# Attention and soft mixture of experts in one kernel: one-operand vector operations, the gate in the norms' rows, four query buffers, a new written order

## The chip, the cores and the metric

One NeuronCore of a Trainium2 chip runs the whole program. The metric is the device time of one execution in microseconds (us), the median of three runs. The engines named below are PE (TensorE: matmuls, and with PEld its weight loads), DVE (VectorE), ACT (ScalarE), POOL (GpSimd) and SP (SyncE, which here only issues DMAs). Each engine works through its own instructions in order and waits where a semaphore tells it to.

## The reference

Batch 8, 8 heads, 576 positions, 64 features a head; then a soft mixture of 8 experts with 4 slots each. All is float32.

```python
scores = softmax_causal(q @ k.T / 8)                     # per (batch, head): 576 x 576
local  = scores @ v
q_p    = phi(q)                                          # phi(x) = x + 1 for x > 0, else exp(x)
mem    = (q_p @ M_prev) / (q_p @ z_prev + 1e-6)
g      = 1 / (1 + exp(-beta))                            # one gate for a head
x      = (g * mem + (1 - g) * local)                     # 4608 rows of 512
logits = x @ phi_moe                                     # 4608 x 32
d      = softmax over the 4608 rows;  slots = d.T @ x    # 32 x 512
slot_out = relu(slots @ w1[e]) @ w2[e]                   # 512 -> 1024 -> 512, per expert
out    = softmax over the 32 slots(logits) @ slot_out    # 4608 x 512
```

## The kernel before

**The attention.** The loop runs over 32 pairs of heads, n = 0 to 31 (8 batches, 4 pairs). A pair's work is cut into small operations, each a function `op_...`. Queries and keys are split on POOL into a rounded part and the rest (`qhi`, `qlo`, `kn`, `kl`, lines 396 to 406). PE multiplies them in three passes (`sA`, `sa`, `sB`, lines 408 to 429). DVE adds the mask and takes the row's extreme (`max`, line 450), ACT makes the exponential with its row sum (`exp`, line 458). PE transposes the blocks (`t`, line 551), ACT or DVE copies them out of PSUM (`te`, lines 364 and 367), and PE multiplies them with v (`av`, line 578).

**The memory branch.** ACT and DVE make phi(q) (`qmin`, `qexp`, `qphi`, lines 488 to 497) in one of three buffers `qp`. PE makes the norms (`norm`, line 503); `neps`, `nmk`, `nred` (lines 508 to 519) turn them into reciprocals, which go by a small DRAM tile `nd` (three of them, used in turn) into 17 rows of a tile `nG`. The row sums are scaled by the gate and inverted by `rec` (lines 464 and 465), transposed (`rt`), and multiplied by `nG` in `rf` (line 473). The product goes through DRAM (`rrw`) and comes back broadcast over 64 partitions as `FR` (`rrr`, line 483). `qn` (line 532) multiplies phi(q) with `FR` before PE uses it in `av.A` and `ava`, and `mo` and `xe` (lines 608 and 613) multiply the result with `FR`'s second half.

**The gate.** ACT makes exp(beta) and exp(-beta) at the start. In DRAM the second half of each `nd` is filled with ones by three DMAs that ACT issues (line 353).

**The first expert steps** run between: `x1` to `x4` (lines 618 to 681) keep a running maximum (`x1m`, line 635), a running denominator (`x1d`, line 648) and the slots' sums (`x4a`) over chunks of 512 rows.

**What sets the order.** `SEQ` (from line 34) writes out all operations in one list by hand or by search; each engine gets its instructions in that list's order and keeps it (`pin`). A table `EV` names the engine of each operation that more than one could do. A helper `turn` (line 843) makes DVE and POOL take turns on eight kinds of operation that read two tensors from SBUF, or feed such ones (`qhi`, `qlo`, `kn`, `kl`, `qphi`, `qn`, `nmk`): where the list goes from one engine to the other, the second waits for the first.

**The tail.** Weights come in pieces of 0.5 MB: 45 during the attention, 19 more when slots of the first layer come free. The first layer (`f1`) is followed by the second (`f2`, line 906), one call for each half of the model's features dh, group of experts and half of the hidden units. Then `comb(dh, t4)` (line 956) multiplies 512 rows with the slots' outputs, ACT and DVE copy the halves out of PSUM (three buffers `pp`), and a DMA writes. Nine blocks of 512 rows are done for dh = 0, then for dh = 1. For the first EARLY = 2 blocks each half of 256 features is written by itself (0.5 MB, line 960); the others are written whole, 1 MB, after dh = 1 (line 962):

```python
    for t4 in range(NQ):
        comb(0, t4)
        if t4 == 4:
            f2(1, 0, 1)
    f2(1, 1, 0)
    f2(1, 1, 1)
```

**The start.** `warm` has PE multiply zeros three times (WARM = 3, line 337) while the first loads are under way.

Of the kernel before, what the change touches and what calls it, by code (L numbers as in the profile page):

```python
# [39 lines left out]
exp.1h0@1 max.4h1@1 te.B3y@0 exp.4h0@1 max.1h1@1 loadq@3 sB@1 te.B3x@0 nrg@1 exp.a@1 te.B3@0 qphi@2 t.B2@0:0 qhi@2  # L40
t.B1@0:1 te.A2@0 te.B2@0 kn@2 max.2h1@1 te.B1@0 norm@2:2 rrr@0 max.2h0@1 qlo@2 exp.2h1@1 av.1@0 max.3h1@1 exp.2h0@1
neps@2 av.3@0 w.r2@0 max.3h0@1 exp.3h1@1 kl@2 av.2@0 exp.1h1@1 av.4@0 exp.3h0@1 nmk@2 exp.4h1@1 sA@2 nred@2 rec@1
nrw@2 sa@2 max.1h1@2 rt@1:0 t.B1@1:1 max.4h1@2 loadk@3 exp.1h1@2 t.B2@1:2 loadv@1 te.B1@1 max.4h0@2 qn.1@0 exp.4h1@2
t.A1@1:1 max.1h0@2 max.a@2 rf@1 sB@2 qn.0@0 rrw@1 te.A1@1 exp.1h0@2 ava@0:0 qmin@3 av.A@0 qhi@3 max.2h1@2 loadq@4
max.3h1@2 te.B2@1 kn@3 nrg@2 t.AA@1:1 xe@0 exp.4h0@2 mo@0 t.A3@1:2 qlo@3 t.A2@1:0 te.AAy@1 qexp@3 te.AAx@1 te.A3@1
t.B3@1:1 max.3h0@2 te.A2@1 kl@3 av.1@1 qphi@3 rrr@1 av.4@1 max.2h0@2 exp.2h1@2 norm@3:0 te.B3x@1 sA@3 exp.2h0@2 neps@3
te.B3@1 nmk@3 exp.3h0@2 te.A3y@1 nred@3 exp.a@2 sa@3 exp.3h1@2 t.A1@2:0 te.B3y@1 nrw@3 max.4h0@3 av.3@1 te.A3x@1
te.A1@2 loadk@4 av.2@1 rec@2 loadv@2 exp.4h0@3 max.1h1@3 rt@2:1 max.a@3 t.B2@2:2 rf@2 exp.1h1@3 max.1h0@3 t.A2@2:0
rrw@2 max.4h1@3 te.B2@2 t.B1@2:1 qn.0@1 qn.1@1 sB@3 loadq@5 te.A2@2 exp.4h1@3 w.r1@0 te.B1@2 ava@1:2 qmin@4 av.A@1
qhi@4 nrg@3 max.3h1@3 kn@4 qexp@4 xe@1 t.AA@2:0 mo@1 t.A3@2:1 qlo@4 exp.a@3 t.B3@2:2 qphi@4 rrr@2 av.1@2 max.3h0@3  # L50
te.B3@2 kl@4 te.B3x@2 max.2h1@3 av.3@2 te.A3y@2 w.r4@0 exp.1h0@3 max.2h0@3 av.2@2 exp.3h1@3 te.A3x@2 te.AAy@2 sA@4
te.A3@2 exp.2h1@3 exp.2h0@3 exp.3h0@3 sa@4 max.1h0@4 norm@4:1 loadk@5 max.1h1@4 te.B3y@2 av.4@2 rec@3 neps@4 loadq@6
t.B1@3:2 te.AAx@2 exp.1h1@4 max.4h0@4 nmk@4 rt@3:1 x3.1@c0:0 te.B1@3 rf@3 qn.0@2 max.4h1@4 exp.1h0@4 rrw@3 t.B2@3:1
x3e.1@c0 t.A1@3:2 max.a@4 nred@4 exp.4h0@4 sB@4 loadv@3 qn.1@2 te.A1@3 te.B2@3 nrw@4 exp.4h1@4 t.A2@3:0 max.2h1@4
qhi@5 qmin@5 ava@2:2 te.A2@3 av.A@2 kn@5 xe@2 exp.a@4 max.2h0@4 exp.2h1@4 t.AA@3:1 mo@2 qlo@5 t.B3@3:0 te.AAy@3
te.AAx@3 x3.0@c0:2 exp.2h0@4 max.3h0@4 rrr@3 t.A3@3:1 te.B3x@3 x3e.0@c0 kl@5 av.1@3 te.A3x@3 te.B3@3 te.A3y@3
max.3h1@4 qexp@5 av.3@3 nrg@4 te.A3@3 sA@5 qphi@5 te.B3y@3 loadv@4 exp.3h0@4 sa@5 w.r5@0 max.1h0@5 exp.3h1@4 norm@5:2
loadk@6 max.4h1@5 av.2@3 loadq@7 neps@5 max.1h1@5 exp.4h1@5 t.B1@4:1 max.a@5 nmk@5 max.4h0@5 t.B2@4:0 te.B1@4 rec@4
t.A1@4:2 qn.1@3 qn.0@3 rt@4:1 sB@5 rf@4 te.A1@4 te.B2@4 rrw@4 qmin@6 nred@5 av.4@3 qhi@6 ava@3:1 av.A@3 exp.4h0@5
max.3h0@5 nrw@5 qlo@6 xe@3 exp.1h1@5 max.2h0@5 w.r0@0 t.A2@4:2 qexp@6 mo@3 loadv@5 t.A3@4:0 exp.2h0@5 t.B3@4:1 kn@6  # L60
max.3h1@5 te.A3@4 av.1@4 te.A2@4 te.A3x@4 kl@6 te.B3x@4 te.A3y@4 exp.3h1@5 x1.0@c0:2 rrr@4 max.2h1@5 exp.a@5 te.B3@4
x1.1@c0 qphi@6 sA@6 x1l@c0 nrg@5 exp.3h0@5 x1m@c0 exp.2h1@5 t.AA@4:0 max.4h1@6 sa@6 te.AAy@4 norm@6:2 exp.1h0@5
loadk@7 av.4@4 max.4h0@6 neps@6 av.2@4 w.r6@0 te.B3y@4 max.a@6 nmk@6 max.1h1@6 te.AAx@4 t.B2@5:2 x1e@c0 max.1h0@6
nred@6 sB@6 exp.4h1@6 rec@5 nrw@6 te.B2@5 x1d@c0 qn.1@4 x2@c0:1 rt@5:0 qn.0@4 t.B1@5:2 av.3@4 rf@5 x2a@c0 max.3h0@6
te.B1@5 rrw@5 x4.0@c0:0 kn@7 qmin@7 max.3h1@6 x3.3@c0:1 qhi@7 x4a.0@c0 exp.1h1@6 ava@4:2 w.r3@0 av.A@4 xe@4 kl@7
exp.3h0@6 x3e.3@c0 loadq@8 exp.4h0@6 max.2h1@6 t.A2@5:0 loadv@6 max.2h0@6 t.A1@5:2 nrg@6 te.A2@5 qlo@7 mo@4 t.A3@5:1
te.A1@5 x3.2@c0:0 te.A3x@5 te.A3@5 t.AA@5:2 te.A3y@5 rrr@5 sA@7 qexp@7 te.AAy@5 x3e.2@c0 te.AAx@5 qphi@7 sa@7
max.1h0@7 exp.2h0@6 t.B3@5:1 loadk@8 max.4h0@7 exp.2h1@6 norm@7:2 av.1@5 max.a@7 neps@7 loadq@9 te.B3x@5 max.4h1@7
exp.3h1@6 nmk@7 av.2@5 max.1h1@7 te.B3y@5 te.B3@5 exp.1h0@6 av.4@5 nred@7 x4.1@c0:0 exp.a@6 exp.4h0@7 sB@7 rec@6 nrw@7
x4a.1@c0 qn.0@5 qn.1@5 rt@6:2 t.B2@6:1 rf@6 exp.1h1@7 t.A1@6:0 max.3h0@7 rrw@6 exp.4h1@7 t.B1@6:2 max.3h1@7 kn@8  # L70
av.3@5 exp.a@7 te.A1@6 qhi@8 av.A@5 exp.3h1@7 te.B2@6 qmin@8 qlo@8 ava@5:0 max.2h1@7 t.A2@6:1 loadv@7 xe@5 te.B1@6
mo@5 t.A3@6:0 nrg@7 exp.2h1@7 kl@8 t.B3@6:2 te.A2@6 exp.1h0@7 av.1@6 max.2h0@7 exp.3h0@7 rrr@6 te.A3x@6 te.B3y@6
te.A3y@6 sA@8 qexp@8 te.A3@6 te.B3@6 qphi@8 t.AA@6:1 sa@8 te.B3x@6 max.1h0@8 t.A1@7:0 exp.2h0@7 loadk@9 max.a@8
max.1h1@8 norm@8:2 max.4h0@8 exp.a@8 av.2@6 loadq@10 te.AAx@6 exp.1h0@8 rec@7 av.4@6 te.A1@7 neps@8 av.3@6 te.AAy@6
nmk@8 max.4h1@8 exp.4h0@8 rt@7:2 x3.1@c1:1 rf@7 t.B1@7:0 exp.4h1@8 nred@8 rrw@7 sB@8 qn.0@6 te.B1@7 x3e.1@c1 qn.1@6
nrw@8 t.A2@7:2 max.3h1@8 qhi@9 w.r8@0 qmin@9 ava@6:1 av.A@6 xe@6 kn@9 max.3h0@8 exp.1h1@8 te.A2@7 t.AA@7:0 mo@6 kl@9
t.A3@7:1 te.AAx@7 qexp@9 t.B3@7:2 te.AAy@7 max.2h0@8 rrr@7 exp.3h0@8 t.B2@7:0 max.2h1@8 qlo@9 av.1@7 te.B3@7 te.A3@7
te.B3x@7 te.B2@7 exp.2h0@8 av.3@7 te.A3y@7 nrg@8 exp.2h1@8 te.A3x@7 sA@9 qphi@9 te.B3y@7 exp.3h1@8 sa@9 max.1h1@9
x3.0@c1:0 loadk@10 max.4h1@9 exp.1h1@9 norm@9:1 loadv@8 x3e.0@c1 av.2@7 max.a@9 max.1h0@9 neps@9 max.4h0@9 t.A2@8:2
exp.4h1@9 nmk@9 rec@8 t.B1@8:0 qn.1@7 qn.0@7 rt@8:1 sB@9 rf@8 te.B1@8 te.A2@8 rrw@8 exp.4h0@9 ava@7:1 nred@9 av.4@7  # L80
qhi@10 av.A@7 qmin@10 max.3h0@9 nrw@9 kn@10 max.2h1@9 t.B2@8:0 qexp@10 loadv@9 qlo@10 xe@7 max.3h1@9 t.A1@8:2 te.B2@8
t.AA@8:1 mo@7 te.A1@8 x1.0@c1:0 kl@10 exp.3h1@9 te.AAx@8 te.AAy@8 x1.1@c1 max.2h0@9 t.A3@8:2 qphi@10 rrr@8 t.B3@8:1
x1l@c1 exp.2h0@9 te.A3y@8 sA@10 x1m@c1 exp.a@9 exp.1h0@9 nrg@9 te.B3y@8 exp.3h0@9 te.A3@8 sa@10 max.1h0@10 norm@10:0
exp.2h1@9 max.4h1@10 av.1@8 loadq@11 te.B3@8 loadk@11 max.1h1@10 te.B3x@8 neps@10 av.3@8 te.A3x@8 max.4h0@10
exp.1h1@10 nmk@10 av.2@8 x1e@c1 max.a@10 nred@10 av.4@8 exp.4h0@10 sB@10 rec@9 nrw@10 qn.0@8 qn.1@8 rt@9:1 x2@c1:0
t.B2@9:2 exp.4h1@10 x2a@c1 rf@9 x4.0@c1:0 max.3h0@10 rrw@9 qhi@11 te.B2@9 av.A@8 max.2h0@10 qmin@11 qlo@11 max.3h1@10
ava@8:2 loadq@12 exp.1h0@10 x4a.0@c1 x3.2@c1:1 loadv@10 xe@8 exp.3h0@10 t.B1@9:0 x3e.2@c1 kn@11 t.A2@9:2 exp.3h1@10
te.B1@9 t.A1@9:1 nrg@10 kl@11 te.A2@9 mo@8 x3.3@c1:0 te.A1@9 t.A3@9:2 max.2h1@10 qexp@11 t.AA@9:1 rrr@9 x3e.3@c1 sA@11
qphi@11 te.AAx@9 te.A3@9 te.AAy@9 sa@11 te.A3x@9 max.1h1@11 norm@11:0 exp.2h1@10 loadk@12 max.4h1@11 av.1@9 exp.2h0@10
# [983 lines left out]
```

## Time and profile before

| what | value |
|---|---|
| three timed runs | 505.86, 508.44, 504.3 us; median 505.86 us |
| the profiled execution | 502.58 us, of which span from first to last instruction 500.8 us |
| mean granted clock of TensorE | 0.951 of full speed |
| busy in the span | PE 440.7 us (88%), DVE 379.6 us (76%), ACT 333.1 us (67%), POOL 186.6 us (37%) |
| DMA | 97.11 MB, mean 194 GB/s |

The busy shares are means over unlike stages: a start in which little is loaded yet, 32 pairs of heads that look alike, an end in which the weights stream in, and a last stretch in which PE has nothing to do and the output is still being written. So the table tells which engine is close to full, and not yet what a change of one stage is worth.

### The profile page before, as it was taken

The page shows a single profiled execution, that of the slowest core. Times are in us where ns is not written, and L with a number is a line of the kernel's source. Part 1 is how long each engine was busy: PE and PEld are TensorE (multiplying, and loading weights), DVE is VectorE, ACT ScalarE, POOL GpSimd, SP SyncE. Part 2 cuts the span into 40 slices and gives each one's busy share as a digit, 9 for nine tenths or more (in the row PEclk, how much of TensorE's full clock was granted, in tenths as well). Part 3 has the DMA queues.
Part 4 walks back from the last instruction along what each step waited for, and adds up shares of the span by engine and source line. Part 5 has one row for each costly group of instructions (what it writes and reads, how often), then busy time and mean ns, then how long its engine had stood idle before and what let it go on. Part 6 is the DMA issues. An engine that isn't in the chain of part 4 may idle for free. (4 is left out here: it accounts for less than half of the span.)

```text
span 500.8 us, 13360 instructions
## 1 busy us (share of the span) xinstructions
PE 440.7 (88%) x4874; PEld 280.8 (56%) x4874; DVE 379.6 (76%) x1229; ACT 333.1 (67%) x956; POOL 186.6 (37%) x196
## 2 busy tenths in 40 slices
...
GB/s 137 84 161 126 264 206 187 193 145 144 135 176 203 177 106 171 134 237 199 174 164 194 168 219 161 175 175 140 239 150 170 131 161 327 394 411 328 21 335 335
DMA packets 40718, 97.11 MB, mean 194 GB/s; under 512 B 9014, under 2 KB 12366, under 8 KB 40654
## 3 DMA queue, kind: packets, MB, share of 16 engines
...
q8 instruction: 38, 0.62, 0.5%
...
## 5 line engine op out<-in xcount | busy, mean ns | idle before, releaser
L458 ACT ACTIVATE sm<-sm,nm 128x576 f32<-128x576 f32 (+4 forms) x288 | 166.3, 580 | 23.0 <-DVE nm L450 22.1
L450 DVE CUSTOM_DVE_ANT_0 sm<-psS,rm 128x192 f32<-128x192 f32 (+4 forms) x288 | 137.3, 509 | 11.8 <-PE psS L424 6.1
L578 PE MATMUL oa<-at,vv 128*32 128x512 f32 (+3 forms) x1280 | 114.9, 469 | 0.2 <-ACT at L364 0.2
L551 PE MATMUL psT<-cs,sm 128*128 128x128 f32 x768 | 109.4, 284 | 5.8 <-DVE rf L473 2.7
L364 ACT COPY at<-psT 128x512 f32<-128x512 f32 (+3 forms) x208 | 84.7, 419 | 42.9 <-PE psT L551 22.2
L551 PEld LDWEIGHTS psT<-cs,sm 128*128 128x128 f32 x768 | 86.1, 144 | 35.9 <-ACT at L364 5.6
L415 PE MATMUL psS<-K,X 64*128 64x256 f32 (+2 forms) x960 | 92.3, 327 | 7.1 <-DVE nm L450 4.8
L415 PEld LDWEIGHTS psS<-K,X 64*128 64x128 f32 x960 | 74.0, 190 | 26.8 <-issue 15.1
L367 DVE COPY at<-psT 128x256 f32<-128x256 f32 (+3 forms) x184 | 82.3, 458 | 8.6 <-ACT at L364 4.6
L532 POOL TENSOR_TENSOR at<-qp,FR 64x576 f32<-64x576 f32 x34 | 48.1, 1416 | 36.0 <-DMA FR<-rd 15.6
L458 ACT ACTIVATION_READ_ACCUMULATOR sm<-sm,nm 128x1 f32 x288 | 54.7, 190 | 0.0
L578 PEld LDWEIGHTS oa<-at,vv 128*32 128x32 f32 x1280 | 35.5, 109 | 31.5 <-issue 19.3
L514 POOL TENSOR_TENSOR rn<-rn,rm 128x144 f32<-128x144 f32 x27 | 11.7, 435 | 109.4 <-DVE rn L510 53.8
L406 POOL TENSOR_TENSOR K<-qk,K 128x576 fp32r<-128x576 f32 x32 | 45.4, 1419 | 3.4 <-DVE qp L497 1.9
L400 POOL TENSOR_TENSOR X<-qk,X 128x512 fp32r<-128x512 f32 x32 | 41.1, 1283 | 0.9
L369 POOL TENSOR_SCALAR X<-qk 128x512 fp32r<-128x512 f32 x32 | 19.9, 620 | 48.2 <-PE psS L415 33.7
L532 DVE TENSOR_TENSOR at<-qp,FR 64x576 f32<-64x576 f32 x30 | 22.3, 743 | 17.5 <-POOL at L532 14.3
L497 DVE SCALAR_TENSOR_TENSOR qp<-qk,qp 128x576 f32<-128x576 f32 x32 | 24.1, 752 | 12.0 <-ACT qp L493 7.3
L488 ACT ACTIVATE qp<-qk 128x576 f32<-128x576 f32 x32 | 21.9, 683 | 14.9 <-DVE at L532 12.3
L608 DVE TENSOR_TENSOR xt<-oa,FR 128x448 f32<-128x448 f32 (+7 forms) x60 | 23.8, 434 | 3.3 <-PE oa L578 3.2
L369 POOL TENSOR_SCALAR K<-qk 128x576 fp32r<-128x576 f32 x32 | 21.6, 675 | 9.0 <-DVE at L532 3.7
L450 DVE DVE_READ_ACCUMULATOR2_ANT nm<- 128x1 f32 x288 | 23.3, 81 | 0.0
...
## 6 DMA issues: line engine op xcount, KB each, us to landing
...
```

Source lines behind the costliest of these rows:

```text
L364: nc.scalar.copy(o, i)
L367: nc.vector.tensor_copy(out=o, in_=i)
L369: ENG = dict(a=act, v=dve, p=lambda o, i: nc.gpsimd.tensor_scalar(out=o, in0=i, scalar1=1.0, scalar2=1.0, op0=ALU.mult, op1=ALU.mult))
L400: nc.gpsimd.tensor_tensor(out=X[:, 1, :], in0=st[n]["q"][:, 64:576], in1=X[:, 0, :].bitcast(F32), op=ALU.subtract)
L406: nc.gpsimd.tensor_tensor(out=K2[:, 1, :], in0=kt[:, 0:S], in1=K2[:, 0, :].bitcast(F32), op=ALU.subtract)
L415: nc.tensor.matmul(ps[h][:, a:e], X[ROW[h], x, 128 * i - 128:128 * i], K2[ROW[h], y, k0:k0 + e - a], start=(x, y) == (0, 0), stop=(x, y) = ...
L450: nc.vector.tensor_tensor_reduce(out=smt(n, i, h), in0=src, in1=msk, op0=ALU.add, op1=ALU.min, scale=-0.125, scalar=3.0e38, accum_out=s["n ...
L458: nc.scalar.activation(sm, sm, AF.Exp, scale=-1.0, bias=s["nm"][:, J:J + 1], accum_out=s["sum"][:, J:J + 1])
L497: ALU_ENG[ev("qphi", n)].scalar_tensor_tensor(out=t, in0=st[n]["q"], scalar=0.0, in1=t, op0=ALU.max, op1=ALU.add)
L532: ALU_ENG[ev(f"qn.{h}", n)].tensor_tensor(out=C[r, h, :], in0=st[n]["qp"][r], in1=FR[r, 0:S], op=ALU.mult)
L551: nc.tensor.transpose(out=ps[:, 128 * x:128 * x + 128], in_=win(n, i, h, c), identity=ident)
L578: nc.tensor.matmul(o[r, c0:c1], vt[:, n % 2, c, r], rhs[h], start=start, stop=stop)
```

## The change

1. Three DVE operations lose one of two tensor operands. `rec` no longer multiplies by the gate (a `tensor_scalar` adds 1e-9). `x1m` and `x1d` take the running value as a per-partition scalar.
2. The gate of the local branch goes into the constant second half of the `nd` tiles, which are now four (one for a pair of heads in the batch). Six more DVE operations of `gate` and four DMAs that SP issues (`ndc`) fill them; ACT's three DMAs at the start are gone.
3. `qp` has four buffers in place of three.
4. WARM is 5, and three `wm` operations put 4 more multiplications of zeros among the first two pairs.
5. EARLY is 4. The `f2` calls of dh = 1 stand after 3, 6 and 9 blocks of dh = 0.
6. `SEQ` and `EV` are written anew. Counted in the two texts: `qn` on DVE 30 times before and 22 after, on POOL 34 and 42; `nmk` on DVE 5 and 1; `neps` on DVE 16 and 19; the copies `te`, `x1l`, `x2a` and `x3e` are shared differently at nearly the same sum. The list goes from POOL to DVE inside `turn` 62 times before and 38 times after; `qphi` on DVE comes directly behind a `qn` on POOL 18 times after and never before. From the last `qn` that frees a buffer to the `qmin` that wants it there were 3 to 19 entries of the list in between, and are 15 to 53.

```diff
-loadq@1 qhi@0 qmin@0 qlo@0 qexp@0 qphi@0 kn@0 gate@0 qmin@1 norm@0:0 neps@0 kl@0 nmk@0 qexp@1 nred@0 qphi@1 nrw@0 sA@0
-sa@0 max.1h1@0 norm@1:1 loadk@1 max.4h0@0 neps@1 loadv@0 max.a@0 max.1h0@0 exp.a@0 max.4h1@0 exp.1h1@0 sB@0 exp.4h1@0
+loadq@1 qhi@0 qlo@0 qmin@0 gate@0 kn@0 qexp@0 kl@0 ndc@0 qphi@0 norm@0:0 sA@0 neps@0 qmin@1 nmk@0 nred@0 qexp@1
+loadv@0 sa@0 max.4h1@0 loadk@1 nrw@0 max.4h0@0 exp.4h1@0 w.r0@0 max.1h0@0 max.1h1@0 loadq@2 exp.1h0@0 max.a@0 wm@2
 ...
-WARM = 3
-EARLY = 2
+WARM = 5
+EARLY = 4
 ...
-    qps = big.tile([128, 3, S], F32, name="qp")
+    qps = big.tile([128, 4, S], F32, name="qp")
 ...
-        for nd in nds:
-            nc.scalar.dma_start(out=nd[:, S:1088].rearrange("h (r x) -> h r x", x=128), in_=nG[0][0:8])
 ...
     def op_gate(n):
-        nc.vector.tensor_scalar(out=omg, in0=omg, scalar1=1.0e20, scalar2=1.0, op0=ALU.min, op1=ALU.add)
-        nc.vector.tensor_scalar(out=gc, in0=gc, scalar1=1.0, scalar2=None, op0=ALU.add)
-        nc.vector.tensor_scalar(out=epg, in0=gc[:, :, 12], scalar1=1e-6, scalar2=None, op0=ALU.mult)
+        nc.vector.tensor_scalar(out=ec, in0=ec, scalar1=1.0e-20, scalar2=None, op0=ALU.max)
+        nc.vector.tensor_scalar(out=epg, in0=ec, scalar1=1e-6, scalar2=None, op0=ALU.mult)
+        nc.vector.tensor_scalar(out=og, in0=og, scalar1=1.0e20, scalar2=1.0, op0=ALU.min, op1=ALU.add)
+        nc.vector.reciprocal(out=og, in_=og)
+        for a, b in ((0, 512), (512, S)):
+            nc.vector.tensor_scalar(out=at[0:8, a:b], in0=acc[0:8, 0:b - a], scalar1=og[0:8], scalar2=None, op0=ALU.add)
+
+    def op_wm(n):
+        ps = psO.tile([128, 512], F32, name="oa")
+        for i in range(n):
+            nc.tensor.matmul(ps, acc[:, 0:128], acc, start=True, stop=True)
+
+    def op_ndc(n):
+        for p in range(NP):
+            nc.sync.dma_start(out=nds[p][:, S:2 * S], in_=at[2 * p:2 * p + 2, 0:S])
 ...
-        nc.vector.scalar_tensor_tensor(out=f, in0=w(st[n]["sum"]), scalar=1e-9, in1=w(omg[:, n % NP, 0:12]), op0=ALU.add, op1=ALU.mult)
+        nc.vector.tensor_scalar(out=f, in0=st[n]["sum"].rearrange("a (h i) -> a h i", i=4), scalar1=1e-9, scalar2=None, op0=ALU.add)
 ...
-        nc.vector.tensor_tensor(out=mn, in0=mo, in1=mx, op=ALU.max)
+        nc.vector.tensor_scalar(out=mn, in0=mx, scalar1=mo, scalar2=None, op0=ALU.max)
 ...
-        nc.vector.scalar_tensor_tensor(out=den, in0=den, scalar=xs[qd]["al"], in1=xs[qd]["sm"], op0=ALU.mult, op1=ALU.add)
+        nc.vector.tensor_scalar(out=den, in0=den, scalar1=xs[qd]["al"], scalar2=xs[qd]["sm"], op0=ALU.mult, op1=ALU.add)
 ...
-    for t4 in range(NQ):
+    for t4 in range(3):
         comb(0, t4)
-        if t4 == 4:
-            f2(1, 0, 1)
+    f2(1, 0, 1)
+    for t4 in range(3, 6):
+        comb(0, t4)
     f2(1, 1, 0)
+    for t4 in range(6, NQ):
+        comb(0, t4)
     f2(1, 1, 1)
```

## Rows read from the trace of the kernel before

**Rows 1.** Windows by stage: busy us (count) of each engine, then PE clock, DMA share, GB/s
```profile
50.00:400.00 350.00, 322.27 (x3700) 212.87 (x3698) 308.60 (x1028) 274.71 (x809) 165.72 (x169) 1.00 0.62 176
456.00:475.70 19.70, 17.00 (x216) 9.34 (x214) 7.43 (x12) 6.68 (x13) 0.00 (x0) 1.00 0.31 112
475.70:500.80 25.10, 9.51 (x60) 6.01 (x58) 5.54 (x8) 4.32 (x8) 0.00 (x0) 0.50 0.92 334
```

**Rows 2.** Window of 4 us inside the last stretch
```profile
480.00:484.00 4.00, 4.00 (x28) 2.61 (x28) 2.08 (x3) 1.76 (x4) 0.00 (x0) 0.50 1.03 375
```

**Rows 3.** Chain that ended last, tail: start us, us, engine and line
```profile
458.41 0.66 PE pp L956 x8
...
463.30 1.86 PE pf L906 x32
465.17 0.66 PE pp L956 x8
...
468.74 3.63 PE pf L906 x64
```

**Rows 4.** Timeline of the start: start us, us, engine, line, operation, [idle before]
```profile
4.42 0.62 POOL L369 TENSOR_SCALAR X<-qk 128x512 fp32r<-128x512 f32 x1 [3.35 <-DMA qk<-in_q_dram]
...
4.83 2.45 ACTq L353 DMA_DIRECT2D nd<-nG  x3
...
7.32 0.68 ACT L488 ACTIVATE qp<-qk 128x576 f32<-128x576 f32 x1 [2.25 <-POOL X L400]
...
9.50 0.18 DVE L378 TENSOR_SCALAR rm<-rm 128x52 f32<-128x52 f32 x1
...
9.67 0.67 POOL L369 TENSOR_SCALAR K<-qk 128x576 fp32r<-128x576 f32 x1 [3.27 <-DVE qp L497]
9.68 0.71 PE L503 MATMUL psT<-qp,qk 128*32 128x144 f32 x8 [3.80 <-issue]
9.81 0.55 DVE L380 TENSOR_SCALAR rm<-rm 128x4 f32<-128x4 f32 x1
...
10.43 1.40 POOL L406 TENSOR_TENSOR K<-qk,K 128x576 fp32r<-128x576 f32 x1
...
11.88 2.02 PE L415 MATMUL psS<-K,X 64*128 64x256 f32 x14 [0.69 <-POOL K L406]
```

**Rows 5.** Window of the start's slow stretch, columns as in the first group
```profile
8.00:22.00 14.00, 10.88 (x64) 7.95 (x64) 8.64 (x31) 7.11 (x21) 4.73 (x6) 0.51 0.25 75
```

**Rows 6.** Single lines: engine, operation, duration ns min/median/max, first and last start
```profile
L464 DVE SCALAR_TENSOR_TENSOR r<-sum,rm x32: 110/171/1155, 23.6 to 401.0; 128x12 f32<-128x12 f32 x32
L648 DVE SCALAR_TENSOR_TENSOR den<-den,al,sm x8: 147/214/4619, 83.1 to 421.2; 128x1 f32<-128x1 f32 x8
L637 DVE TENSOR_SCALAR nmn<-mrun x8: 153/154/155, 80.0 to 417.0; 128x1 f32<-128x1 f32 x8
```

**Rows 7.** Timeline around the longest of line 648
```profile
171.10 4.62 DVE L648 SCALAR_TENSOR_TENSOR den<-den,al,sm 128x1 f32<-128x1 f32 x1
...
174.30 1.40 POOL L406 TENSOR_TENSOR K<-qk,K 128x576 fp32r<-128x576 f32 x1
```

**Rows 8.** Window behind it, columns as in the first group
```profile
172.00:180.00 8.00, 4.29 (x67) 3.06 (x66) 7.93 (x17) 3.77 (x12) 3.70 (x4) 0.92 0.04 6
```

**Rows 9.** Waits, summed: who waited for whom, us in total, times, longest
```profile
ACT qp L488 <- DVE at L532: 12.3, 12, 2.6
```

**Rows 10.** Groups by shape: xcount, busy us, mean ns, idle before
```profile
L532 POOL TENSOR_TENSOR at<-qp,FR 64x576 f32<-64x576 f32 x34 | 48.1, 1416 | 36.0 <-DMA FR<-rd 15.6 <-DVE nm L450 5.9 <-DVE r L464 4.4
L532 DVE TENSOR_TENSOR at<-qp,FR 64x576 f32<-64x576 f32 x30 | 22.3, 743 | 17.5 <-POOL at L532 14.3 <-DMA FR<-rd 2.8
L464 DVE SCALAR_TENSOR_TENSOR r<-sum,rm 128x12 f32<-128x12 f32 x32 | 10.4, 326 | 3.2 <-ACT sm L458 3.0
L337 PE MATMUL psT<-acc 128*128 128x512 f32 x6 | 4.4, 897 | 1.4 <-DVE acc L333 1.4
```

502 lines of the change are left out of this document (250 added, 252 removed).

## The prediction

> **What bounds the kernel now.** I read the stages first, then the tail's chain, the start's timeline, and last the small DVE operations one by one.
>
> In the windows by stage [rows 1] see three regimes. From 50 to 400 us PE is busy 322.27 of 350 us (92%) at full granted clock, DVE 308.60 (88%), POOL 165.72 (47%). PE's work is the same after the change, so at most its 27.7 us of idle time can be won there, and DVE is close enough to full that each stall of DVE can become one of PE. From 456 to 475.7 the DMA engines are busy 0.31 of the time. In the last 25.1 us PE has nothing left after 9.51 us: the output is being written, 334 GB/s x 25.1 us = 8.38 MB, which is 7 blocks of 1.05 MB and two halves; once it runs, the write holds 375 GB/s with the DMA share at its top [rows 2]. So the end is set by what is still to be written when dh = 1 begins, and the middle by PE with DVE close behind.
>
> **The change part by part.** The sum is against the profiled execution, 502.58 us, which lies 3.3 us under the median of the three runs, 505.86.
>
> *Tail writes (EARLY 4).* Two more halves of 0.52 MB are written during dh = 0, when the DMA engines are mostly free [rows 1]; four halves at 375 GB/s are 5.6 us and fit between the first block at 458.41 and 475.7 [rows 1, 3]. What remains is 7.34 MB, so 1.05 MB / 375 GB/s = 2.8 us off the end. PE makes a half each 9.51/9 = 1.1 us in that stretch [rows 1], 0.52 MB in 1.1 us being more than the DMA takes, so the supply doesn't limit. The new homes are pieces whose weights were used by the f2 calls of dh = 0; no wait is added. Bounds -1.5 (if two blocks must first collect) to -3.2 (at 334 GB/s). **-2.8.**
>
> *f2 between the blocks.* Five blocks took 463.30 - 458.41 = 4.89 us, four 468.74 - 465.17 = 3.57 [rows 3]: 0.94 a block, where the first of a group takes 0.66 of PE and the rest waits for copies. An f2 of 1.86 us [rows 3] lets all three PSUM buffers empty. Three groups of three at four fifths of 0.94 are 6.8 us, at 0.89 8.0, against 8.46. **-0.7**, bounds 0 and -1.7. It moves the first write of dh = 1, so it counts in full.
>
> *Start.* ACT issues three DMAs from 4.83 to 7.28 and its first `qmin` stands behind them until 7.32, though the query was there at 4.42 [rows 4]. That goes. But what is late next is POOL: in the new list the four splits come before `qphi`, so they end at about 4.42 + 0.62 + 1.40 + 0.67 + 1.40 = 8.5 (taking `qlo` as long as `kl`) instead of 11.83, and `qphi` waits for them by `turn`, with six small operations of the gate ahead of it on DVE (0.18 each [rows 4], so up to 1.1, and two longer ones that no row shows; 0 if they get done under POOL's work). With 0.74 for `qphi` from the nearest row [rows 10] and 0.71 for `norm` [rows 4] the scores start at 10.0 to 11.1, and all 18 passes, at 2.02/14 each, end at 12.6 to 13.7, against 13.9. The four `ndc` DMAs stand ahead of `loadv`, `loadk` and `nrw` on SP; at 2.45/3 each [rows 4] they cost SP 3.3 us, before any of those is wanted (`nrw` after `nred`, behind `norm`).
> The clock is the larger part. From 8 to 22 us it is granted at 0.51, the lower level of 1.2 GHz, after 3.80 us in which PE had nothing [rows 4, 5]. Two more multiplications of zeros ahead, 4.4/3 = 1.5 us each [rows 10], fill most of that gap and delay nothing. If the clock then stays at 2.4 GHz, 10.88 us of PE work become 5.4, a gain of up to 5.4 where PE is what is waited for. The four others cost up to 5.9 us at the lower clock, covered by the 3.1 us that PE is idle in that window: +2.8 if the clock stays low. Between -6.7 and +2.8 I take **-2**, nearer the row with the gap that gets filled, cut because DVE and ACT work 8.64 and 7.11 of those 14 us.
>
> *Small DVE operations.* The same `x1d` that takes 214 ns at the median took 4619 once [rows 6]: it began at 171.10 and ended at 175.72, when POOL's four splits in a row ended (174.30 + 1.40) [rows 7]. Behind it PE was busy 4.29 of 8 us where 92% would be 7.4, and the clock dropped to 0.92 [rows 8]: 3.1 us lost. `rec` has a median of 171 and a mean of 326 [rows 6, 10], so 32 x 0.155 = 5.0 us of DVE time stands behind POOL. With one tensor operand both should go: 0 to -8.1. Against it speaks line 380, which has one tensor operand and 4 columns: it took 0.55 us and ended at 10.36, with POOL's copy (9.67 + 0.67), while line 378 with 52 columns took 0.18 before POOL was at work [rows 4]. The Trainium skill ("SBUF — State Buffer", section "Who interferes with whom") says that a `tensor_scalar` between SBUF operands can enter a mode that uses both ports, and then contends with GpSimd all the same. By that rule this term would be 0 for `rec`; line 380 agrees with it. `x1d` and `x1m` have one element; the one-element operation of line 637 took 153 to 155 ns [rows 6], and no row shows it beside POOL. So I keep the 3.1 of the long stall and leave `rec`'s 5.0 for the range: **-3.**
>
> *Order, engines, buffers.* In DVE's stretch 8 `qn` less are 8 x 0.743 = 5.9 us, and its 14.3 us of waits for POOL's `qn` [rows 10] should shrink with 38 handovers in place of 62; together some 20 us. The moved `nmk`, `neps` and copies are between 0.18 and 0.74 us each and nearly cancel. Four buffers remove ACT's 12.3 us of waits for `qn` [rows 9]; ACT isn't full, so this counts only where an exponential behind it is late. POOL gets 8 x 1.416 = 11.3 us, on 47%. How much of DVE's 20 us reaches PE no row shows: at most all, at least less than nothing (second rival). I take a fifth, since PE idles only 8% of this stage: **-4**, bounds -12 and +13. The early weight loads lie on DMA engines that are busy 0.62 [rows 1] and count nothing; without that cover each would delay a small transfer by 0.52 MB / 375 GB/s = 1.4 us.
>
> **Sum:** -2.8 - 0.7 - 2 - 3 - 4 = -12.5: 490.1 on the profiled execution, **493.4 us** on the median.
>
> **The rivals.**
> 1. *The order carries nothing, nor does the start.* PE at 92% is close to its bound, and what DVE saves may only lengthen its idle time. Then only the tail is left: 505.86 - 3.5 = 502.4. For it: PE's share; against it: the 24 handovers less.
> 2. *Slower: POOL paces.* `qphi` on DVE now comes directly behind a POOL `qn` 18 times. POOL's `qn` waits for `FR` from DRAM, 15.6 us in all [rows 10], and takes 1.416 where DVE takes 0.743. All of DVE's queue, the `max` that free the scores' PSUM and half of the copies, then stands behind `qphi`. 18 x 1.42 = 25.5 us of DVE held up, and if half reaches PE +12.8; with the tail and the start, 505.86 + 12.8 - 5.5 = 513.2. It decides from about 0.6 us a time, 11 us. Against it: POOL's 47%.
> 3. *The port stays taken.* The one-operand forms wait for POOL as line 380 did, and a long stall falls somewhere else: the 3 us term is 0, 496.4. For it line 380 [rows 4], against it that only 1 of 8 `x1d` hit POOL's long row.
> 4. *The order frees more.* DVE's 20 us come through at over half: -12 for -4, 485.4.
>
> **How the numbers follow.** What a measurement of this kernel can't tell from no change is about 1%, 500.8 to 510.9. Forecast 0.42 (488 to 500), rival 1 0.17, rival 2 0.13, rival 3 0.13, rival 4 0.15. Faster: 0.42 + 0.13 + 0.15 = 0.70; the same 0.17; slower 0.13. The range leaves out rival 2 and the lower half of rival 4: 485 to 505, with the upper end taking in rival 1 and 2.6 us of scatter of the runs.
>
> **What would show it.** Tail: four 0.5 MB writes before the last f2, and a last stretch of some 22 us. Start: the granted clock from 8 to 22 us near 1, the scores of the first pair done before 13.9. Small operations: no `x1d` over 0.3 us beside POOL; if `rec`'s mean stays near 0.33 the third rival holds for it. Order: PE above 93% in the pairs' stage, DVE's waits for POOL under 14 us; more than 11 us of waits of `qphi` for POOL would be the second rival. Wrong altogether if PE's share in that stage falls.

## The result

The changed kernel takes 471.65 us in the median of four runs (469.84 to 473.24), the kernel before on the same chip 505.31 (504.3 to 508.44): a ratio of 0.9323, 95% interval 0.9268 to 0.9378. The forecast was 493.4 with a range of 485 to 505. The profiled execution of after took 471.04 us (span 469.2, mean granted clock 0.981).

Where it went follows from marks that both traces have. The reciprocal of the row sums (`rec`) of the second pair starts at 36.00 us before and 32.04 after: 4.0 us from the start. From there to the same mark of the last pair it is 365.21 and 340.12 us: 25.1 us from thirty pairs. From the first layer's first matmul to the end of the span it is 72.7 and 70.0 us: 2.7 us from the tail.

Windows by stage of after, columns as in [rows 1], answer to [rows 5] (start), the first row of [rows 1] (pairs) and its last (from the first write of dh = 1 on, which is at 446.06 here and at 475.66 before):

```profile
8.00:22.00 14.00, 11.31 (x87) 6.51 (x85) 7.95 (x29) 8.59 (x25) 4.96 (x6) 1.00 0.51 151
50.00:400.00 350.00, 337.49 (x3968) 222.10 (x3970) 307.09 (x1055) 279.03 (x832) 177.18 (x179) 1.00 0.66 194
446.06:469.20 23.14, 6.21 (x60) 3.43 (x59) 5.25 (x8) 4.36 (x8) 0.00 (x0) 0.68 0.89 318
```

See the second row: PE is busy 337.49 of 350 us, 96.4% in place of 92.1. Between the two marks of `rec`, PE's gaps sum to 8.5 us (29.7 before), and its busy time falls from 335.5 to 331.6. The first row has the granted clock at 1.00 where [rows 5] had 0.51.

The groups by shape of after that answer to [rows 10] (xcount, busy us, mean ns, idle before), and the single line of `x1d` that answers to [rows 6]:

```profile
L540 POOL TENSOR_TENSOR at<-qp,FR 64x576 f32<-64x576 f32 x42 | 59.5, 1416 | 88.2 <-DMA FR<-rd 65.2 <-DVE qp L505 6.4 <-PE psT L477 5.8
L540 DVE TENSOR_TENSOR at<-qp,FR 64x576 f32<-64x576 f32 x22 | 16.5, 748 | 5.9 <-POOL at L540 4.2 <-DMA FR<-rd 1.5
L472 DVE TENSOR_SCALAR r<-sum 128x12 f32<-128x12 f32 x32 | 4.8, 150 | 5.2 <-ACT sm L467 4.8
L656 DVE TENSOR_SCALAR den<-den,al,sm x8: 215/263/270, 94.6 to 398.1; 128x1 f32<-128x1 f32 x8
```

DVE now stands 5.9 us ahead of its `qn` (17.5 before), while POOL waits 65.2 us for `FR` (15.6 before): the wait for the landing has moved to the engine that has time. `rec` takes 150 ns (326), and no `x1d` takes over 270 (one took 4619).

The share of the chain that ended last, by line, from the page of after:

```profile
PE oa L586 12%; PE psT L559 11%; PE psS L424 11%; DMA FR<-rd 8%; DVE sm L459 5%; PE pf L898 3%; DVE at L364 3%; PE pf L915 3%; ACT sm L467 2%; POOL at L540 2%; PE pp L965 2%; PE psT L672 2%; ACT at L361 2%; DMA qk<-in_k_dram 2%; DVE qp L505 2%
```

Beside PE's three large lines stands one transfer, `FR`, with 8%, some 38 us, though PE is busy 92% of the span. The runs of group 7 below come from this row.

### The profile page after: what moved, and what is told of

The parts are those of the page before. It is cut to its first block, busy times and chain, and to the rows that moved or that the text cites. A ratio compares the mean times of both kernels' runs of the same rounds, so it can differ in the third digit from the quotient of the medians.

```text
span 469.2 us, 13385 instructions
## 1 busy us (share of the span) xinstructions
PE 430.6 (92%) x4886; PEld 272.8 (58%) x4886; DVE 364.9 (78%) x1223; ACT 329.4 (70%) x953; POOL 199.5 (43%) x208
## 4 chain that ended last, share of the span: by engine, by line
PE 53%; DVE 15%; DMA 11%; ACT 6%; POOL 6%; issue 3%; SPq 1%; POOLq 0%; DVEq 0%; ACTq 0%
PE oa L586 12%; PE psT L559 11%; PE psS L424 11%; DMA FR<-rd 8%; DVE sm L459 5%; PE pf L898 3%; DVE at L364 3%; PE pf L915 3%; ACT sm L467 2%; POOL at L540 2%; PE pp L965 2%; PE psT L672 2%; ACT at L361 2%; DMA qk<-in_k_dram 2%; DVE qp L505 2%
## 5 line engine op out<-in xcount | busy, mean ns | idle before, releaser
L467 ACT ACTIVATE sm<-sm,nm 128x448 f32<-128x448 f32 (+4 forms) x288 | 166.6, 582 | 27.4 <-DVE nm L459 26.4
L459 DVE CUSTOM_DVE_ANT_0 sm<-psS,rm 128x448 f32<-128x448 f32 (+4 forms) x288 | 137.5, 508 | 5.5 <-PE psS L424 2.7
L586 PE MATMUL oa<-at,vv 128*32 128x512 f32 (+3 forms) x1280 | 117.8, 469 | 2.8 <-ACT at L361 1.2
L559 PE MATMUL psT<-cs,sm 128*128 128x128 f32 x768 | 106.9, 278 | 1.6 <-ACT at L361 0.7
L540 POOL TENSOR_TENSOR at<-qp,FR 64x576 f32<-64x576 f32 x42 | 59.5, 1416 | 88.2 <-DMA FR<-rd 65.2
L364 DVE COPY at<-psT 64x256 f32<-64x256 f32 (+3 forms) x189 | 83.0, 450 | 10.1 <-ACT at L361 4.4
L424 PE MATMUL psS<-K,X 64*128 64x256 f32 (+2 forms) x960 | 88.4, 320 | 2.6 <-DVE nm L459 2.0
L424 PEld LDWEIGHTS psS<-K,X 64*128 64x128 f32 x960 | 70.9, 185 | 21.9 <-issue 7.8
L366 POOL TENSOR_SCALAR X<-qk 128x512 fp32r<-128x512 f32 x32 | 19.9, 622 | 47.6 <-PE psS L424 19.2
L505 DVE SCALAR_TENSOR_TENSOR qp<-qk,qp 128x576 f32<-128x576 f32 x32 | 23.9, 748 | 9.5 <-POOL at L540 4.0
L501 ACT ACTIVATE qp<-qp 128x576 f32<-128x576 f32 x32 | 21.8, 683 | 0.4
L496 ACT ACTIVATE qp<-qk 128x576 f32<-128x576 f32 x32 | 21.7, 677 | 0.2 <-DMA qk<-in_q_dram 0.2
L540 DVE TENSOR_TENSOR at<-qp,FR 64x576 f32<-64x576 f32 x22 | 16.5, 748 | 5.9 <-POOL at L540 4.2
(171 smaller groups left out, 469.2 us busy)
```

The source lines that it names most:

```text
L364: nc.vector.tensor_copy(out=o, in_=i)
L366: ENG = dict(a=act, v=dve, p=lambda o, i: nc.gpsimd.tensor_scalar(out=o, in0=i, scalar1=1.0, scalar2=1.0, op0=ALU.mult, op1=ALU.mult))
L424: nc.tensor.matmul(ps[h][:, a:e], X[ROW[h], x, 128 * i - 128:128 * i], K2[ROW[h], y, k0:k0 + e - a], start=(x, y) == (0, 0), stop=(x, y) = ...
L459: nc.vector.tensor_tensor_reduce(out=smt(n, i, h), in0=src, in1=msk, op0=ALU.add, op1=ALU.min, scale=-0.125, scalar=3.0e38, accum_out=s["n ...
L467: nc.scalar.activation(sm, sm, AF.Exp, scale=-1.0, bias=s["nm"][:, J:J + 1], accum_out=s["sum"][:, J:J + 1])
L505: ALU_ENG[ev("qphi", n)].scalar_tensor_tensor(out=t, in0=st[n]["q"], scalar=0.0, in1=t, op0=ALU.max, op1=ALU.add)
```

## The experiments

Times are medians; ratios are to the kernel before on the same chip. That kernel's own median lay between 504.7 and 507.6 us from chip to chip, so differences of under 2 us between runs that did not share a chip say nothing.

### 1. The order alone: the list and table of before in the changed kernel

```diff
-SEQ, EV of the changed kernel
+SEQ, EV of the kernel before, with "ndc@0" after "gate@0", "wm@2" before "sB@0", "wm@1" before "norm@1" and before "sA@1"
```

> The changed kernel with the list SEQ and the table EV of before (the gate's writes put in after the gate, the three groups of zeros at like places); four buffers, one-operand operations, gate in the rows and the new tail stay. The profiles put the gain at -4 us before the second pair, -25 in pairs 2 to 31, -2.8 in the tail. Theory order (the new list and table carry what the pairs gained, because DVE no longer stands behind POOL's qn): 492 to 500 us; DVE's idle time ahead of L540 back near 17 us, PE's gaps of over 0.3 us between 36 us and the last reciprocal back near 20 us in sum. Theory operands (the removed second operands carry it, the stall behind x1d above all): 475 to 481 us, PE's gaps near 5 us. Theory buffers (four buffers carry it whatever the list): 475 to 481 us, with qmin never waiting.

493.1 us (0.9767, 0.9700 to 0.9834), inside the order theory's window. So 21.5 of the 33.7 us hang on the list and the table, and the theories of operands and of buffers fall as the main cause. Between the marks of `rec`, PE's gaps of over 0.3 us are 18.9 us in sum, and DVE stands longer ahead of its `qn` than in the kernel before (17.5):

```profile
L540 DVE TENSOR_TENSOR at<-qp,FR 64x576 f32<-64x576 f32 x30 | 22.5, 749 | 21.7 <-POOL at L540 19.6 <-DMA FR<-rd 1.7
```

The same stretch between the marks of `rec`, with the old list and with the new one, columns as in [rows 1]:

```profile
31.68:395.37 363.69, 339.78 (x3839) 223.60 (x3838) 313.81 (x1078) 285.31 (x842) 172.11 (x176) 0.99 0.62 175
32.04:372.16 340.12, 331.62 (x3858) 218.87 (x3856) 308.33 (x1070) 283.39 (x840) 185.15 (x187) 1.00 0.65 185
```

Of the 23.6 us between the two, 15.4 are gaps of PE and 8.2 are its busy time, which is longer with the old list at a slightly lower granted clock; why it is longer was not taken apart.

The timeline around its second longest gap of PE (start us, us, engine, line, operation, [idle before]):

```profile
315.10 0.34 SPq L403 DMA_DIRECT2D vv<-in_v_dram  x1
315.25 0.75 DVE L616 TENSOR_TENSOR xt<-oa,FR 128x128 f32<-128x128 f32 x2
315.50 0.42 SPq L698 DMA_DIRECT2D w<-in_w_dram  x1
316.10 1.35 SPq L491 DMA_DIRECT2D FR<-rd  x2
...
325.21 1.40 POOL L540 TENSOR_TENSOR at<-qp,FR 64x576 f32<-64x576 f32 x1 [3.06 <-DMA FR<-rd]
326.65 0.75 DVE L540 TENSOR_TENSOR at<-qp,FR 64x576 f32<-64x576 f32 x1 [3.07 <-POOL at L540]
327.32 0.27 DVE L481 TENSOR_TENSOR rf<-psT,nG 24x128 f32<-24x128 f32 x1
327.65 0.32 PE L586 MATMUL psT<-at,vv 128*32 128x64 f32 x8 [2.78 <-DVE rf L481]
```

Read it upwards. PE stood 2.78 us for `rf`, a small operation of DVE whose input had been there since 324.0. `rf` stands in DVE's queue behind DVE's `qn`, which waits by `turn` for POOL's, and that waits for `FR`, whose read was issued 9.1 us earlier, right behind a weight's 0.5 MB and a v load. That read itself could only go out when `mo` of the pair before (315.25) was through with the tile. `rf` itself adds little here: the matmul that stood for it also multiplies what DVE's `qn` writes (`at`), and that was done at 327.40, 0.19 us ahead of `rf`.

The same pair in the changed kernel with its own list:

```profile
300.29 0.74 DVE L616 TENSOR_TENSOR xt<-oa,FR 128x128 f32<-128x128 f32 x2
301.05 1.14 SPq L491 DMA_DIRECT2D FR<-rd  x2
...
306.88 0.28 DVE L481 TENSOR_TENSOR rf<-psT,nG 24x128 f32<-24x128 f32 x1 [0.16 <-PE psT L477]
307.02 1.41 POOL L540 TENSOR_TENSOR at<-qp,FR 64x576 f32<-64x576 f32 x1 [2.70 <-DMA FR<-rd]
...
309.25 0.76 DVE L540 TENSOR_TENSOR at<-qp,FR 64x576 f32<-64x576 f32 x1
```

The read follows `mo` in the same way, and POOL waits 2.70 us for it; from issue to POOL's `qn` it takes 5.97 us in place of 9.11. On DVE `rf` now stands ahead of `qn` and has 0.16 us to wait, for PE; and when DVE comes to its `qn`, POOL's is done. The matmul that needs both `qn` starts at 310.55, after other work of PE and without a wait.

### 2. The operands alone

```diff
+    ones12 = const.tile([128, 12], F32, name="ones12")
-nc.vector.tensor_scalar(out=f, in0=sum, scalar1=1e-9, ...)
+nc.vector.scalar_tensor_tensor(out=f, in0=sum, scalar=1e-9, in1=ones12, op0=ALU.add, op1=ALU.mult)
 ... (x1m, x1d likewise with two tensors)
```

> The changed kernel with two tensor operands again in rec (times a tile of ones), x1m and x1d; everything else as changed. Theory order: 473 to 477 us (rec's mean near 0.3 us in place of 0.150, one to three stalls of 0.3 to 4 us beside POOL). Theory operands: 490 us or more, with PE gaps of 20 us and more in sum again. Theory buffers: under 475 us.

476.87 us (0.9434, 0.9360 to 0.9507): 5.2 us slower. `rec` is back at a mean of 303 ns with a longest of 1251, `x1d` at 875 at most; none hit a long row of POOL's work in the new list. The other way round, one operand in the kernel before:

```diff
-nc.vector.scalar_tensor_tensor(out=den, in0=den, scalar=al, in1=sm, op0=ALU.mult, op1=ALU.add)
+nc.vector.tensor_scalar(out=den, in0=den, scalar1=al, scalar2=sm, op0=ALU.mult, op1=ALU.add)
 ... (x1m likewise; rec with one operand, its gate left out)
```

> The kernel before with one-operand rec, x1m and x1d and nothing else (the local branch's gate is left out, since rec carried it). Theory operands: 490 to 497 us. The forecast's term, the long stall of x1d alone: 501 to 503. Theory order: 500 to 504, since what DVE saves goes into its waits for POOL's qn.

498.36 us (0.9882, 0.9838 to 0.9927), 6.7 less than 505.05, between the windows of two theories. In both lists the operands are worth 5 to 7 us. The lines of `rec` and `x1d` in this run, to set beside [rows 6]:

```profile
L464 DVE TENSOR_SCALAR r<-sum x32: 106/160/167, 23.2 to 396.4; 128x12 f32<-128x12 f32 x32
L648 DVE TENSOR_SCALAR den<-den,al,sm x8: 201/262/273, 82.4 to 416.7; 128x1 f32<-128x1 f32 x8
```

### 3. Where qn runs

```diff
+EV.update({"qn.0@...": ...})   # after: each qn on the engine it had before (30 DVE, 34 POOL)
+EV.update({k: "p" for k in EV if k.startswith("qn.")})   # before: all 64 on POOL
```

> The changed kernel with the new list, but each qn on the engine that it had before (30 on DVE, 34 on POOL, in place of 22 and 42). Theory engine (where qn runs is what frees DVE and so PE): 483 to 492 us, DVE idle ahead of L540 10 us or more. Theory lead (the list puts the query branch half a pair earlier, so the landing of FR no longer stands before DVE's qn, whichever engine has it): 472 to 476 us, DVE idle ahead of L540 under 8 us. Theory operands: 472 to 476 us too, but then the run with two operands is slow.

481.54 us (0.9515, 0.9435 to 0.9594): 9.9 us slower, just under the window of the engine theory, far over that of the lead. Eight more `qn` on DVE are 8 x 0.748 = 6.0 us of its busy time; that the rest is waiting was not shown.

> The kernel before with all 64 qn on POOL and nothing else changed, so that no FR's landing and no POOL qn can stand ahead of DVE through a qn of its own. Theory engine: 485 to 497 us, PE's gaps of over 0.3 us under 15 us in sum (25.5 before). Theory lead: 503 to 510 us: PE waits for the late qn itself, since the list keeps the landing late and POOL's qn takes over 1.4 us where DVE's takes less. Theory operands: within 2 us of before.

504.62 us (1.0039, 0.9990 to 1.0089): nothing. The handovers from POOL to DVE fall from 62 to 36 here, as few as in the new list, so their number isn't the cause. Two `qn` one after the other on POOL (2 x 1.41 us) keep PE and then `mo` and `xe`:

```profile
L609 DVE TENSOR_TENSOR xt<-oa,FR 128x448 f32<-128x448 f32 (+7 forms) x60 | 23.8, 435 | 11.6 <-PE oa L579 11.3
L614 DVE TENSOR_TENSOR xt<-psT,FR 128x64 f32<-128x64 f32 x32 | 7.0, 219 | 12.3 <-PE psT L579 12.1
```

They have 23.9 us of idle time together ahead of them, 3.7 in the kernel before. So moving `qn` off DVE gains in the new list and not in the old: a property of the list, not of the engine.

### 4. The query branch's place

In the list, each operation of the branch (`qmin` to `nrw`) of pairs 3 to 30 was shifted by half a pair of PE's work; `norm` took a free PSUM slot.

```diff
-... sA@10 ... with qmin@10 30 entries ahead of sA@10, norm@10 10 behind
+... sA@10 ... with qmin@10 65 entries ahead of sA@10, norm@10 32 ahead
```

> The changed kernel with the list and table of before (the run that took 493.1 us), in which alone the query branch (qmin, qexp, qphi, norm, neps, nmk, nred, nrw) of pairs 3 to 30 is moved ahead by half a pair, to where the new list has it (qmin 12 units ahead of its pair's scores in place of 5, new list 15; a pair is 16). Engines as before; handovers from POOL to DVE 55 for 62, of them 24 between two qn (26). Theory lead (the earlier branch is what the new list wins): 477 to 486 us. Theory handover of qn (a qn of DVE behind POOL's qn, 26 times before and 12 after, is what costs): 490 to 497, since those stay. Theory operands can't tell it from 493.

> The changed kernel with its own list, in which alone the query branch of pairs 3 to 30 is moved back by half a pair, to where the list of before had it (qmin 6 units ahead of its scores; nrg moved back with it by 5). Between two qn there are now 8 handovers (12 in the changed kernel), but 30 qphi on DVE stand behind POOL's splits as before. Theory lead: 482 to 493 us. Theory handover of qn: 469 to 475 us.

535.84 us (1.0628, 1.0585 to 1.0671) and 520.96 us (1.0320, 1.0280 to 1.0361): 43 and 49 us slower than the kernels that they were made from, outside every window, and so neither tells for or against the lead. The rows show why: the branch was moved, its loads were not.

```profile
L497 ACT ACTIVATE qp<-qk 128x576 f32<-128x576 f32 x32 | 21.7, 678 | 14.8 <-DMA qk<-in_q_dram 14.8
```

```profile
L511 PE MATMUL psT<-qp,qk 128*32 128x144 f32 x256 | 14.6, 300 | 15.0 <-DMA qk<-in_q_dram 12.2 <-DVE qp L505 1.2 <-PE psT L336 0.9
```

In the first run ACT stands 14.8 us ahead of `qmin` for a query that isn't there yet (0.2 in the changed kernel), in the second PE stands 12.2 us ahead of `norm`. What the lead is worth by itself stays open.

### 5. Buffers, zeros, tail

```diff
-qps = big.tile([128, 3, S], F32, name="qp")   # before, with n % 3
+qps = big.tile([128, 4, S], F32, name="qp")   # n % 4
```

> The kernel before with four qp buffers in place of three, nothing else. ACT's 12.3 us of waits of qmin for qn go in either case. Theory buffers: 490 to 500 us. Every other theory: 503 to 507 us, since ACT is busy 67% and the list is what it was.

504.56 us (0.9995, 0.9961 to 1.0028). Buffers alone are worth nothing. The new list has `qmin` ten sixteenths of a pair earlier, so it may need them; with three buffers it was not run.

```diff
-WARM = 5, wm@2, wm@1, wm@1
+WARM = 3
```

> The changed kernel with 3 multiplications of zeros at the start as before and none among the first pairs. Theory clock (the zeros keep TensorE's clock at 2.4 GHz from 8 to 32 us, and that is most of the 4 us won before the second pair): clock at half over some 10 us and more before 32 us, 474 to 478 us. Rival (the start was won by the new order and ACT's three DMAs that went): 470 to 473 us, with the clock at half and nothing lost by it.

476.14 us (0.9428, 0.9391 to 0.9465): 4.5 us slower, and the mark of the second pair is at 35.97 in place of 32.04. The zeros alone are the start's gain. The same window without them (clock 0.63, fewer matmuls done):

```profile
8.00:22.00 14.00, 8.93 (x61) 6.69 (x62) 7.37 (x26) 6.59 (x20) 4.07 (x6) 0.63 0.49 151
```

```diff
-EARLY = 4; f2 after 3, 6 and 9 blocks
+EARLY = 2; f2(1, 0, 1) after the fifth block, the others after the ninth
```

> The changed kernel with EARLY 2 and the f2 calls of the second half of the features where they stood before. The forecast's two terms of the tail, 2.8 and 0.7 us: 474 to 476 us. By the profiles, 2.8 between the first layer's start and the end: 474.4.

474.93 us (0.9388, 0.9317 to 0.9460): 3.3 us slower.

The four parts taken out one at a time, 21.5 + 5.2 + 4.5 + 3.3 = 34.5, give the whole 33.7 within the scatter.

### 6. The landing of FR and the turns of qn

```diff
     def op_rrr(n):
+        if n > 0:
+            return
```

> The changed kernel with the list and table of before (493.1 us), in which FR is read back from DRAM for the first pair only: the reads rrr of the other pairs are left out, so qn, mo and xe multiply with the first pair's values. No qn waits for a landing any more; all engines' work and the handovers by turn stay. Theory landing (DVE stands behind POOL's qn because that waits for FR): 474 to 484 us, DVE idle ahead of L540 under 8 us in place of 21.7. Theory handover (POOL's qn of 1.41 us itself is what DVE stands behind): 486 to 493, DVE idle there still over 12 us. Theory balance (no single wait; the whole list): 487 to 495.

> The changed kernel with its own list, FR read back for the first pair only (rrr of the other pairs left out, as in the run beside it). Theory landing: 468 to 472 us, since the new list has little left of that wait (DVE idle ahead of L540 5.9 us), so that the distance to the list of before shrinks from 21.5 us to under 12. Theory handover and theory balance: the same here, but the distance stays over 15.

Both kernels leave out the reads, so that every pair is multiplied with the first pair's `FR`. 473.6 us (0.9397, 0.9342 to 0.9453) with the list of before and 464.63 (0.9225, 0.9155 to 0.9294) with the new one, 0.4 and 3.4 us under the landing theory's windows. Without the landings the old list gains 19.5 us, the new one 7.0, and 9.0 of the 21.5 us between them are left. What goes with the reads is more than one wait: their issues and waits in SP's queue go too, and with the old list the DMA share from 50 to 350 us falls from 0.63 to 0.44. The runs with the split read (group 7) keep the traffic. DVE's wait ahead of `qn` with the old list:

```profile
L542 DVE TENSOR_TENSOR at<-qp,FR 64x576 f32<-64x576 f32 x30 | 22.5, 750 | 5.8 <-POOL at L542 5.2
```

5.8 us, which is what the new list has with its landings in place: the landing theory, by its number.

```diff
-f in ("qhi", "qlo", "kn", "kl", "qphi", "qn", "nmk")
+f in ("qhi", "qlo", "kn", "kl", "qphi", "nmk")
```

> The changed kernel with the list and table of before (493.1 us), in which qn is taken out of the operations that DVE and POOL do in turn: DVE's qn waits for FR but no longer for POOL's qn, and the two may run at once. Theory handover: 474 to 485 us. Theory landing: 488 to 494, since FR's landing is awaited by both (DVE idle ahead of L540 by DMA in place of by POOL). A rival of both: two qn at once slow each other so that DVE's takes over 1 us in place of 0.75, 493 to 500.

The helper's list has seven kinds of operation, not eight; here `qn` leaves it. 485.22 us (0.9633, 0.9566 to 0.9700), 7.9 us less, just outside the handover theory's window and under the landing theory's.

```profile
L540 DVE TENSOR_TENSOR at<-qp,FR 64x576 f32<-64x576 f32 x30 | 26.4, 880 | 6.9 <-DMA FR<-rd 6.6
L540 POOL TENSOR_TENSOR at<-qp,FR 64x576 f32<-64x576 f32 x34 | 49.3, 1449 | 39.0 <-DMA FR<-rd 32.5 <-PE psT L559 2.5 <-PE psS L433 1.5
```

The means (880 for 749 ns, 1449 for 1415) mix two cases. By the starts and ends in the trace only 11 of DVE's 30 `qn` met one of POOL's; these took 1114 ns on average (685 to 1794) and POOL's 1523, the other 19 took 745 and POOL's 1414. Nine of the 11 ended 592 to 618 ns after POOL's, however early they had begun: they stood until POOL was through, as in the turns. Still 21.7 us of DVE's idle time become 6.9.

> The list and table of before in the changed kernel (493.1 us) with both removals together: FR read back for the first pair only (19.5 us less by itself) and qn out of the turns of DVE and POOL (7.9 less by itself). If both removals take away the same wait (DVE's qn behind a POOL qn that waits for the landing): 470 to 475 us, no sum of the two. If they are two waits that add: 464 to 468.

474.19 us (0.9347, 0.9299 to 0.9395), no less than without the landings alone. It is one wait: with the landing gone, `qn` behind `qn` costs nothing that can be told.

### 7. From the cause to a faster kernel

```diff
-        for h in range(2):
-            nc.sync.dma_start(out=FR[ROW[h]], in_=rd[h:h + 1].broadcast_to([64, 2 * S]))
+        for c in (0, S):
+            for h in range(2):
+                nc.sync.dma_start(out=FR[ROW[h], c:c + S], in_=rd[h:h + 1, c:c + S].broadcast_to([64, S]))
```

> The changed kernel with FR read back in two halves, first the one that qn needs, then the one that mo and xe need. The first no longer waits until mo and xe of the pair before are through with the second (24.1 us of waits in 23 times in the queue of SP). Theory landing: part of the 7 us that the run without the reads showed to be left, 466 to 470 us. Rival: two more issues a pair on SP delay what stands behind, 472 to 476.

465.73 us (0.9186, 0.9141 to 0.9232), faster than forecast for it and 1.5% under the changed kernel by the ratios, whose intervals don't meet.

```profile
L541 POOL TENSOR_TENSOR at<-qp,FR 64x576 f32<-64x576 f32 x42 | 59.5, 1417 | 52.3 <-DMA FR<-rd 31.8 <-DVE qp L506 9.2 <-PE psT L560 4.6
L541 DVE TENSOR_TENSOR at<-qp,FR 64x576 f32<-64x576 f32 x22 | 16.4, 746 | 1.4 <-POOL at L541 1.2
```

POOL's wait for `FR` is halved, DVE's idle time ahead of `qn` falls from 5.9 to 1.4 us, and the chain that ended last (from the page, as above) has `FR` with 5% in place of 8:

```profile
PE psT L560 13%; PE oa L587 13%; PE psS L424 12%; DMA FR<-rd 5%; DVE sm L459 5%; PE pf L899 3%; ACT sm L467 3%; PE pf L916 3%; DVE at L364 2%; PE psT L673 2%; ACT at L361 2%; PE pp L966 2%; PE psT L633 2%; PE psT L512 1%; PE psS L433 1%
```

The trace has both an earlier issue and a shorter way. Over pairs 4 to 29 the read that `qn` needs is issued 0.79 us before `mo` and `xe` of the pair before have ended (0.08 us after it in the changed kernel), and over pairs 3 to 29 its 128 packets have ended 3.41 us after the issue (4.70 for the whole read). Which of the two gains was not taken apart.

> The kernel before with FR read back in two halves (qn's first) and nothing else. Theory landing (the old list loses its time to the landing of FR, which waits for mo and xe of the pair before): 488 to 497 us. If the landing is late in the old list for another reason (rec and rf late, the way through DRAM): 500 to 507.

494.16 us (0.9792, 0.9718 to 0.9866), 10.6 us under the kernel before, by two more DMA issues a pair (four in place of two) and nothing else. DVE's idle time ahead of `qn` falls from 17.5 to 8.0 us.

> The changed kernel with qn out of the turns. Theory landing: the new list has only 4.2 us of DVE's waits for POOL's qn left, so 468 to 473 us. Theory handover: 462 to 467, by the 18 qphi and 12 qn that no longer wait. Rival: operations at once on both engines slow each other, 473 to 478.

468.22 us (0.9258, 0.9192 to 0.9324), 0.7% under the changed kernel by the ratios, with intervals that overlap.

> The changed kernel with FR in two halves and qn out of the turns, each of which alone gained (465.7 and 468.2 us against 471.7). One wait taken away twice: 464 to 467 us. Two waits that add: 460 to 463.

464.18 us (0.9172, 0.9131 to 0.9214): with the split, the turns add nothing that can be told. It is the fastest kernel that leaves nothing out, level with 465.73.

## Why the prediction was wrong

**The term that failed** is "order, engines, buffers": "How much of DVE's 20 us reaches PE no row shows [...] I take a fifth, since PE idles only 8% of this stage: -4, bounds -12 and +13." It measured 21.5 us, beyond the term's own bound of -12. The share was reasoned from an average. PE's 29.7 us of gaps were not spread: 25.5 us lay in 33 gaps of over 0.3 us, and of the five longest (3.71 to 1.97 us) the first stood behind the stall of `x1d`, the other four all led back to DVE's `qn`: in two PE waited for `rf`, which stood behind it in DVE's queue, and in two its next matmuls multiply what `qn` writes. So in these gaps DVE's wait [rows 10] did not lie beside PE's idle time, it was PE's. Following PE's five longest gaps back would have shown that. That the result lies near DVE's 20 us doesn't mean that all of these came through: DVE's idle time ahead of `qn` fell by 11.6 us (17.5 to 5.9), and 9.0 of the 21.5 us stay when the landings are taken out, from a cause that stays open (in the new list alone the engines of `qn` are worth 9.9). Nor was PE's work the same, as the prediction had it: its busy time fell from 335.5 to 331.6 us.

**What I did not see** is a loop. `FR` is one tile. Its read waits until `mo` and `xe` of the pair before are through, `qn` waits for the read, PE for `qn`, and `mo` for PE. Mean us a pair, from the starts and ends of those lines, pairs 3 to 29:

| | before | changed, old list | changed |
|---|---|---|---|
| read issued to first qn | 5.92 | 5.99 | 5.10 |
| first qn's start to both ends | 2.69 | 2.68 | 3.10 |
| to the end of mo and xe | 3.43 | 3.31 | 3.11 |
| to the next read's issue | 0.25 | 0.25 | 0.08 |
| a pair | 12.29 | 12.23 | 11.39 |

The four stretches follow one another, so they add up to a pair in any case, and the sum alone proves nothing. What speaks for a loop is that nearly nothing lies between them: the read is issued 0.25 or 0.08 us after `mo` and `xe`, and in the new list POOL stood idle for `FR` ahead of 21 of these 27 first `qn`. In the two old lists that was so for 7 of 27, and for 11 and 14 POOL came to `qn` straight from its other work; so there POOL's own queue had a part in the pace. The new list makes the way round 0.8 us shorter, 30 times, most of it between the read's issue and `qn`. Half of that is a quicker read (5.13, 5.14 and then 4.70 us from the issue to its last packet), half a POOL that stands ready when `FR` lands (from there to `qn` 0.79, 0.86 and then 0.40 us). That cutting the loop gains was shown by the runs of groups 6 and 7.

What made single landings late was only read from the traces: over pairs 3 to 29 of the three together the way from issue to `qn` was 5.26 us on average for the 37 reads with no 0.5 MB weight issued in the 6 us ahead, and 7.67 (5.96 to 9.12) for the eight with one in the last 1.5 us. The forecast had costed those loads at nothing. But the new list has two such reads and the old one three, so they alone are not what it gains.

**Point by point.** *Tail*, -3.5: 3.3 by the run. Four halves are issued from 431.11 to 435.86, before the last `f2` at 440.79. The stretch from the first write of dh = 1 took 23.1 us against 25.1, not the 22 forecast: it ran at 318 GB/s on average, where it had run at 334 before. From the first layer's start to that write it took 46.9 against 47.6 (-0.7 forecast for the `f2` between). *Start*, -2: 4.5, all of it the zeros; the clock near 1 was forecast, its full worth was not believed. *Small operations*, -3: 5.2 and 6.7. The stall of `x1d` went as said, and `rec`'s part, left for the range, came too. *Order*: above.

**The rivals.** The first (nothing from order and start) fell. The second fell: `qphi` waited 4.0 us for POOL's `qn`, 7 times, where 11 would have decided. The third fell: seven of 32 `rec` ran beside POOL's work and took 107 to 160 ns, as the others did. The Trainium skill's rule ("SBUF — State Buffer", section "Who interferes with whom"), that a `tensor_scalar` between SBUF operands can enter a mode that uses both ports and then contends with GpSimd, does not show in these rows. In the gate's operation, 8x512 and then 8x64 with one tensor operand, it may (timeline of after):

```profile
4.82 1.65 DVE L380 TENSOR_SCALAR at<-acc,rm 8x512 f32<-8x512 f32 x2
5.09 1.33 POOL L409 TENSOR_TENSOR X<-qk,X 128x512 fp32r<-128x512 f32 x1
```

The second of the two, 8x64, took 1249 ns, where the larger first took 474, and ended at 6.47, just behind POOL's 6.42, as line 380 of before ended with POOL's copy [rows 4]. So some one-operand operations may be held up and others not; what sets them apart was not tested. For `rec` and `x1d` the measurement decides: the stall was gone. The fourth, that the order frees more, was right in kind and half the size: 12 forecast for it, 21.5 measured.
